# Scores paired by key halves of one sequence, the rows of odd heads by 64x64 quarters, one product with values moved a step forward

## The chip, the cores and the metric

One core of one Trainium2 chip. The metric is the time of one execution on the device in microseconds. Engine names are those of the profile: PE (TensorE matmuls, PEld its weight loads), DVE (VectorE), ACT (ScalarE), POOL (GpSimd), SP (SyncE, which issues DMAs here).

## The reference

Attention in which each score row keeps only the keys within `tau` of its maximum, then a mixture of experts in which each token goes to one expert. 8 batches, 8 heads, 576 positions, head size 64; 4608 tokens of width 512, 8 experts, hidden size 1024.

```python
scores = scale * np.matmul(q, k.transpose(0, 1, 3, 2))
scores = np.where(scores >= scores.max(-1, keepdims=True) - tau, scores, -1e9)
attn = softmax(scores)                       # over 576 keys
x = (attn @ v), heads side by side           # 4608 x 512
e_idx = argmax(x @ w_gate); gate_w = softmax(x @ w_gate)[e_idx]
out[token] = gate_w * sigmoid(x @ w_output_gate)[e_idx] * (relu(x @ w1[e_idx]) @ w2[e_idx])
```

## The kernel before

**Units and steps.** A unit `u` is one head of two sequences (`a` = 0, 1): 32 units. Two units, an even one and an odd one, make a group of nine steps (`STEPS`), 16 groups in all; step `t` of a group stands below as step 0 to 8. A step takes 128 queries of both sequences: steps 0 to 3 the four blocks of the even unit, steps 5 to 8 those of the odd unit, and step 4 the last 64 queries of both units and both sequences (`u is None` in the code).

**What a step does on each engine.** Step `g` issues, in an order that is written out in `Attention.run` and kept on PE, DVE, ACT and POOL:

- PE: the scores of step `g` into two PSUM tiles `ps[0]`, `ps[1]` (one for each sequence; a tile has two banks, and the two key halves `hf` of 288 keys lie in one bank each); in steps 0 and 4 the rows (`x_rows`: a finished head's output turned back to tokens, with the router's two products, 80 columns); in steps 1, 2, 3, 5, 6, 7, 8 a share of the product with values (`av_units`; ten products per head and half, shared out by the table `AV`); then the transposes of the probabilities of step `g - 2` (`remainder`, 2 products, and `blocks`, 16).
- DVE: two drains of the scores (L151, one for each sequence: scaled scores to SBUF, with the row extreme), then two masks of step `g - 1` (L178: threshold, product with the exponentials, row sums).
- ACT: two exponentials (L163), then the copies out of PSUM: the transposes of `remainder` (L229, L222) and of `blocks` (L254, in the step that transposes step 4's probabilities L248 and L250), the values' product (`X<-pa`, L273), in steps 0 and 4 the rows (L310, L312) between and after the exponentials.
- POOL: the threshold of the step (L156), sums, the rows' scaling (L322, L331), the router's scatters.

PSUM is full: `ps` has four banks and is used anew in every step, `pt` (the `blocks` transposes, L243) two banks and `pa` and `pr` one bank each, all in a single buffer. So PE's scores of a step wait for the drains of the step before, its `blocks` for ACT's copy of the last `blocks`, and a new product with values for ACT's copy of the last one.

**Operands.** fp32 products run as two passes. Queries and keys of a unit lie in one SBUF tile `qk`: sequence 0 on partitions 0 to 63, sequence 1 on partitions 64 to 127, so the two products that run side by side in the two row halves of the array are those of the two sequences, and both score tiles are finished at the end of the step's scores. `qk` has three buffers (`LB`), 608 KB each, loaded by one DMA on SP's queue, nine steps ahead.

**After the attention** the experts run on PE (lines from L968 on) with weights that SP's queue loads; eight of these loads are issued during the attention.

Of the kernel before, what the change touches and what calls it, by code (L numbers as in the profile page):

```python
# [8 lines left out]
F32 = mybir.dt.float32  # L9
# [12 lines left out]
class Attention:  # L22
    WU = 7
    SB = 4
    PB = 3
    LB = 3
    VB = 4
    STEPS = 9
    ENDS = 4
    WARM = {0: 4, 1: 2}  # L30
    AV = {1: (1, 0, 5), 2: (1, 5, 8), 3: (1, 8, 10), 5: (0, 0, 2), 6: (0, 2, 5), 7: (0, 5, 8), 8: (0, 8, 10)}
    PLACE = (2, 7)
    ROUTE = (2, 3, 6, 7, 8)

    def __init__(self, ctx, tc, ident, qkv, tau, wg, shape, router):
        self.tc, self.nc = tc, tc.nc
        nc = self.nc
        self.qkv = qkv
        self.B, self.H, self.S, self.D = shape
        self.NB = self.S // P  # L40
        self.M = self.NB * P
        self.R = self.S - self.M
        self.HS = self.S // 2
        self.KP = self.S + self.R
        self.QA = 2 * P
        self.NK = 2 * self.NB + 1
        self.nu = self.B // 2 * self.H
        self.router = router
        pool = lambda name, bufs, **kw: ctx.enter_context(tc.tile_pool(name=name, bufs=bufs, **kw))
        self.ld = pool("ald", self.LB)  # L50
        self.sp = pool("asp", 3)
        self.const = pool("aconst", 1)
        self.vld = pool("avld", self.VB)
        self.w2 = pool("aw2", 1)
        self.w3 = pool("aw3", 3)
        self.xp = pool("axp", 1)
        self.ps_s = pool("ps_s", 2, space=PSUM)
        self.ps_t = pool("ps_t", 1, space=PSUM)
        self.ps_a = pool("ps_a", 1, space=PSUM)
        self.ps_r = pool("ps_r", 1, space=PSUM)  # L60
        c = self.const
        self.ident = ident
        self.tau = c.tile([P, 1], F32, name="tau_sb")
        self.tau_in, self.wg_in = tau, wg
        warm = c.tile([P, 1], F32, name="warm")
        nc.vector.memset(warm, 0.0)
        nc.scalar.activation(warm, warm, AF.Exp)
        E2 = wg.shape[2]
        self.XW = self.D + E2
        self.wx = c.tile([P, self.H, self.XW], F32, name="wx")  # L70
        self.X = [c.tile([P, self.S + 64 * (1 - i)], F32, name=f"X{i}") for i in range(2)]
        self.half = [slice(0, 64), slice(64, P)]
        for pp in self.half:
            nc.gpsimd.tensor_copy(
                self.wx[pp, :, 0 : self.D], ident[pp, None, pp].broadcast_to([self.D, self.H, self.D])
            )
        nc.gpsimd.memset(self.X[0][0:64, self.S :], 0.0)
        self.loaded, self.sums, self.rinv, self.lt, self.sumup = {}, {}, {}, {}, None
        self.PTa, self.PTb, self.slot = {}, {}, 0

    def load_qk(self, u, first=False):
        nc, QW = self.nc, self.S
        x = self.ld.tile([P, QW + self.KP], F32, name="qk")
        src = self.qkv[u]
        if first:
            nc.sync.dma_start(x[:, QW:], src[:, QW : QW + self.KP])
            nc.sync.dma_start(x[:, 0:P], src[:, 0:P])
            nc.sync.dma_start(x[:, P:QW], src[:, P:QW])
        else:
            nc.sync.dma_start(x, src[:, 0 : QW + self.KP])  # L90
        self.loaded[u] = [x[:, 0:QW], x[:, QW:]]

    def load_v(self, u):
        v = self.vld.tile([P, self.NB * P + P], F32, name="vld")
        self.nc.sync.dma_start(v, self.qkv[u][:, self.S + self.KP :])
        self.loaded[u].append(v)

    def warm_up(self, n):
# [21 lines left out]
    def where(self, g):  # L120
# [2 lines left out]
            return s, None, self.NB  # L123
        return s, 2 * s + (i > self.ENDS), i - (self.ENDS + 1) * (i > self.ENDS)

    def scores(self, g, ps):
        nc, (s2, u, t) = self.nc, self.where(g)
        S, HS = self.S, self.HS
        c0 = 512 - HS
        for hf in range(2):  # L130
            cs = slice(c0 + hf * HS, c0 + hf * HS + HS)
            ks = lambda k0: slice(k0 + hf * HS, k0 + hf * HS + HS)
            if u is None:
                for i in range(2):
                    q, k = self.loaded[2 * s2 + i][0:2]
                    for a, pp in enumerate(self.half):
                        nc.tensor.matmul(
                            ps[i][self.half[a ^ i], cs], q[pp, self.M :], k[pp, ks(self.R * a)], start=True, stop=True
                        )
            else:  # L140
                q, k = self.loaded[u][0:2]
                for a, pp in enumerate(self.half):
                    nc.tensor.matmul(  # L143
                        ps[a][:, cs], q[pp, t * P : t * P + P], k[pp, ks(self.R * (1 - a))], start=True, stop=True
                    )
        mn = self.w3.tile([P, 2], F32, name="mn", bufs=4)
        ss = []
        SC = -(self.D ** -0.5)
# [106 lines left out]

    def av_units(self, u):
        nc = self.nc
        v = self.loaded[u][2]
        vm = v.rearrange("p (k a d) -> p k a d", a=2, d=64)
        X = self.X[u % 2]  # L260
        for half in range(2):
# [28 lines left out]
    def x_rows(self, u):  # L290
        X, pp, W, h = self.X[u % 2], self.half, self.XW, u % self.H
        ps = [pool.tile([P, 512], F32, name=name) for pool, name in ((self.ps_a, "pa"), (self.ps_r, "pr"))]
        mm = lambda out, c0, n, a: self.nc.tensor.matmul(
            out, X[pp[a], c0 : c0 + n], self.wx[pp[a], h], start=True, stop=True
        )
        last = slice(self.NB * W, self.NB * W + W)
        if u % 2:
            for a in range(2):
                mm(ps[0][pp[a], last], self.M, 64, a)
        for j in range(self.NB):  # L300
            for a in range(2):
                mm(ps[a][:, j * W : j * W + W], j * P, P, a)
        if u % 2 == 0:
            for a in range(2):
                mm(ps[a][:, last], self.M - 64 * a, P, a)
        return ps

    def x_copy(self, u, px, out, xl, a):
        nc, W = self.nc, self.XW
        nc.scalar.copy(xl[:, a::2], px[a][:, 0 : (5 - a) * W].rearrange("p (j w) -> p j w", w=W))  # L310
        if a and u % 2 == 0:
            nc.scalar.copy(xl[64:P, 8], px[1][64:P, 4 * W : 5 * W])  # L312
        if out:
            out(a)
# [32 lines left out]
    def run(self, hooks, begun):  # L347
# [4 lines left out]
        self.prep_first()  # L352
        for g in range(G + self.ENDS + 1):
            s, t = divmod(g, T)
            if t in (0, self.ENDS + 1) and s + 1 < ns:
                nxt = 2 * s + 2 + (t > 0)
                self.load_qk(nxt)
                self.load_v(nxt)
            g2 = g - 2
# [71 lines left out]
class Router:  # L431
# [71 lines left out]
    def init_units(self):  # L503
# [5 lines left out]
        for dst, group in parts:  # L509
            for r in range(0, dst.shape[0], P):  # L510
                ins = self.nc.sync.dma_start(dst[r : r + P, :], self.zrow)
                self.nodep(ins, group)
                self.init.append(ins)
                yield False

# [671 lines left out]
def lay_out(q, k, v, wg, wog):  # L1187
# [10 lines left out]
    vr = np.zeros((n, 2, r, 2, d), np.float32)  # L1198
    for a in range(2):
        vr[:, a, :, a] = vt[:, a, m:]  # L1200
    rows = lambda x: x.reshape(n, 2 * d, -1)
    qkv = np.concatenate(
        [rows(qt), rows(kt[..., m:]), rows(kt), vm, vr.reshape(n, 2 * r, 2 * d)], axis=2
    )
    e = wg.shape[1]
    w = np.zeros((2, d, h, 2, e), np.float32)
# [27 lines left out]
```

## Time and profile before

| | |
|---|---|
| median of 3 runs | 950.47 us (950.23 to 950.50) |
| profiled execution | 952.78 us, of which the span is 951.1 us |
| busy: PE, DVE, ACT, POOL | 98%, 71%, 64%, 33% of the span |
| granted clock of TensorE | 0.997 of full speed |
| attention | about the first 476 us |

The profiled execution is 2.3 us above the median of the runs; the span is that from its first to its last instruction. PE stands at 98%, but the ends of matmuls are modelled, so a busy PE also covers the time in which a product drains or the array changes its form. What the engines wait for is read from the waits and from the times at which instructions start.

### The profile page before, as it was taken

To read this page: it belongs to the slowest core of one execution; us is meant where nothing else is said; L and a number is where in the kernel's file an instruction comes from. 1 tells how busy PE (TensorE), PEld (TensorE's weight loads), DVE (VectorE), ACT (ScalarE), POOL (GpSimd) and SP (SyncE) were. 2 spreads that over 40 slices of the span, in tenths; PEclk is the share of its full clock that TensorE was granted. 3 is DMA by queue.
4 is the path that set the end of the run, shared out by engine and by line. 5 is a ranking of instruction groups with operands and counts; after the bars stand their busy time and mean duration, and the time that the engine had idled before them with its cause. 6 is when DMAs were issued, how large, how long until landed. Compare 5 with 4: busy or idle time off the path is not lost. (4 is left out here: it accounts for less than half of the span.)

```text
span 951.1 us, 21910 instructions
## 1 busy us (share of the span) xinstructions
PE 933.5 (98%) x8329; PEld 680.9 (72%) x8329; DVE 674.9 (71%) x1605; ACT 611.7 (64%) x1211; POOL 317.4 (33%) x568
## 2 busy tenths in 40 slices
PE   8999999999999999999999999999999999999996
PEld 4666666665666656666678887778878878878885
DVE  7899999999999999999965753435535535536621
ACT  6899898898988989889863332424424434436521
POOL 4344343456634576447626310202002002002001
PEclk9999999999999999999999999999999999999998
DMA  8972112123321233212247852526526426527301
GB/s 267 289 262 82 58 66 82 42 82 108 116 82 41 82 115 108 83 42 86 91 150 242 284 184 71 178 89 220 175 89 232 163 87 241 167 89 258 132 22 45
DMA packets 71402, 126.14 MB, mean 133 GB/s; under 512 B 8703, under 2 KB 35583, under 8 KB 71296
## 3 DMA queue, kind: packets, MB, share of 16 engines
q1 hardware_dynamic: 64656, 103.71, 34.3%
q0 software_dynamic: 6640, 21.02, 5.7%
q8 instruction: 66, 1.08, 0.5%
q14 instruction: 40, 0.33, 0.1%
HBM read 95.26 MB, written 30.22 MB: 132 GB/s over the span
## 5 line engine op out<-in xcount | busy, mean ns | idle before, releaser
L163 ACT ACTIVATE p<-s,mn 128x576 f32<-128x576 f32 x288 | 213.5, 782 | 45.3 <-DVE s L151 43.8
L178 DVE SCALAR_TENSOR_TENSOR p<-s,thr,p 128x576 f32<-128x576 f32 x288 | 231.2, 839 | 1.9 <-POOL thr L156 1.9
L151 DVE TENSOR_SCALAR_CACHE_REDUCE s<-ps 128x576 f32<-128x576 f32 x288 | 206.2, 753 | 33.2 <-PE ps L143 31.1
L1019 ACT ACTIVATE hh<-ph 128x512 fp32r<-128x512 f32 (+2 forms) x96 | 49.2, 512 | 205.1 <-PE ph L1016 199.8
L156 POOL TENSOR_SCALAR thr<-mn,tau_sb 128x2 f32<-128x2 f32 x144 | 97.5, 677 | 193.0 <-DVE s L151 190.0
L143 PE MATMUL ps<-qk 64*128 64x288 f32 x1024 | 155.9, 418 | 0.0
L1020 DVE SCALAR_TENSOR_TENSOR hl<-ph,hh 128x512 fp32r<-128x512 f32 (+2 forms) x96 | 55.5, 578 | 139.9 <-ACT hh L1019 136.5
L1014 PE MATMUL ph<-xh,w1h 128*128 128x512 f32 (+2 forms) x384 | 136.0, 354 | 0.0
L1016 PE MATMUL ph<-xh,w1l 128*128 128x512 f32 (+2 forms) x384 | 133.5, 348 | 0.2 <-issue 0.2
L1015 PE MATMUL ph<-xl,w1h 128*128 128x512 f32 (+2 forms) x384 | 133.4, 347 | 0.2 <-DVE xl L823 0.2
L1036 PE MATMUL py<-w2h,hh 128*128 128x512 f32 x304 | 120.3, 396 | 0.9 <-ACT hh L1019 0.9
L1038 PE MATMUL py<-w2h,hl 128*128 128x512 f32 x304 | 120.5, 396 | 0.6 <-DVE hl L1020 0.6
L811 POOL DMA_INDIRECT out_dram<-yo,kid x39 | 42.7, 1095 | 233.0 <-DVE yo L810 86.7
L1037 PE MATMUL py<-w2l,hh 128*128 128x512 f32 x304 | 120.0, 395 | 0.0
L269 PE MATMUL pa<-PTb,vld 128*64 128x320 f32 x640 | 101.3, 444 | 2.2 <-ACT X L273 1.5
L143 PEld LDWEIGHTS ps<-qk 64*128 64x128 f32 x1024 | 92.1, 188 | 14.5 <-DVE s L151 1.9
L243 PE MATMUL pt<-ident,p 64*128 64x64 f32 x2304 | 96.6, 223 | 3.5 <-ACT PTb L254 1.8
L243 PEld LDWEIGHTS pt<-ident,p 64*128 64x128 f32 x2304 | 83.5, 139 | 6.0 <-ACT PTb L254 4.9
L1014 PEld LDWEIGHTS ph<-xh,w1h 128*128 128x128 f32 x384 | 72.1, 188 | 11.9 <-issue 0.8
L823 DVE TENSOR_TENSOR w1l<-r,w1h 128x1024 fp32r<-128x1024 f32 x52 | 63.7, 1225 | 22.8 <-ACT w1h L820 21.9
L269 PE MATMUL pa<-PTa,vld 128*64 128x256 f32 x640 | 79.7, 387 | 0.0
L1015 PEld LDWEIGHTS ph<-xl,w1h 128*128 128x128 f32 x384 | 72.2, 188 | 10.1 <-DVE xl L823 0.6
(199 smaller groups left out, 1514.7 us busy)
## 6 DMA issues: line engine op xcount, KB each, us to landing
r<-in_moe_w_dram SPq DMA_DIRECT2D x104, 512.0 KB, 4.1
qk<-in_qkv_dram SPq DMA_DIRECT2D x31, 608.0 KB, 3.9
vld<-in_qkv_dram SPq DMA_DIRECT2D x32, 320.0 KB, 3.7
xs<-zrow SPq DMA_DIRECT2D x32, 257.0 KB, 8.2
xg<-xs SPq DMA_DIRECT2D x6, 1028.0 KB, 5.2
xg<-xs SPq DMA_DIRECT2D x4, 514.0 KB
xg<-xs SPq DMA_DIRECT2D x2, 771.0 KB
out_dram<-yo,kid POOLq DMA_INDIRECT x39
```

Of the source, the lines that this page charges most:

```text
L143: nc.tensor.matmul(ps[a][:, cs], q[pp, t * P : t * P + P], k[pp, ks(self.R * (1 - a))], start=True, stop=True)
L151: nc.vector.tensor_scalar(s, ps[a][:, c0 : c0 + S], SC, None, op0=ALU.mult, op1=ALU.min, accum_out=mn[:, a : a + 1])
L163: self.nc.scalar.activation(e, s, AF.Exp, bias=mn[:, a : a + 1], scale=-1.0)
L178: nc.vector.scalar_tensor_tensor(e, s, thr[:, a : a + 1], e, op0=ALU.is_le, op1=ALU.mult, accum_out=sums[a])
L243: nc.tensor.transpose(pt[:, o : o + 64], p[hs[h], k0 : k0 + P], id_[hs[h], hs[h]])
L269: nc.tensor.matmul(pa[self.half[a], 0:N], vm[:, kb, a], PT[:, 4 * a + kb if i else self.NK - 1], start=(i == 0), stop=(i == self.NB), skip ...
L1014: nc.tensor.matmul(ph, w1h[:, c, fs], self.xh[:, c, 0:N], start=(c == 0), stop=False)
L1015: nc.tensor.matmul(ph, w1h[:, c, fs], self.xl[:, c, 0:N], start=False, stop=False)
L1016: nc.tensor.matmul(ph, w1l[:, c, fs], self.xh[:, c, 0:N], start=False, stop=(c == 3))
L1036: nc.tensor.matmul(Y, hh[:, ts], wh, start=(f == 0), stop=False)
L1037: nc.tensor.matmul(Y, hh[:, ts], wl, start=False, stop=False)
L1038: nc.tensor.matmul(Y, hl[:, ts], wh, start=False, stop=(f == 7))
```

## The change

Six edits. (1) Each unit's queries are laid out twice, on both partition halves, and its keys by halves: key half 0 on partitions 0 to 63, key half 1 on 64 to 127. The two products that run side by side are now the two key halves of one sequence, and sequence 0's scores come before sequence 1's. (2) `qk` grows to 928 KB and has two buffers, and each unit is loaded five steps before its first use, not nine (`nxt`). The first unit is loaded in six pieces. (3) The rows of odd heads are made by products of 64 tokens, four quarters of the array side by side (20 products of 64x64 in place of 2 of 64x64 and 8 of 64x128), and their last 64 tokens of sequence 1 now need a copy of their own on ACT, as those of even heads do (L312). (4) `AV`: step 5 makes three of the ten steps of a head's first half and step 6 two; before it was two and three. (5) The zero rows that the router's buffer is filled with (`xs<-zrow`, 32 DMAs) each wait for a threshold on POOL, which spreads them over steps. (6) The layout of the input follows on the host.

```diff
-    LB = 3
+    LB = 2
-    AV = {1: (1, 0, 5), 2: (1, 5, 8), 3: (1, 8, 10), 5: (0, 0, 2), 6: (0, 2, 5), 7: (0, 5, 8), 8: (0, 8, 10)}
+    AV = {1: (1, 0, 5), 2: (1, 5, 8), 3: (1, 8, 10), 5: (0, 0, 3), 6: (0, 3, 5), 7: (0, 5, 8), 8: (0, 8, 10)}
...
+        b = [0, P, P + KH, S + KH, S + KH + P, self.QK - KH, self.QK]
+        for i in (1, 0, 5, 3, 2, 4) if first else ():
+            nc.sync.dma_start(x[:, b[i] : b[i + 1]], src[:, b[i] : b[i + 1]])
...
+    def operands(self, u, a, pp, q0, k0):
+        x, S, KH = self.loaded[u][0], self.S, self.KH
+        n = min(P, S - q0)
+        q0 += a * (S + KH) + (KH if q0 and not a else 0)
+        k0 += self.QK - KH if a else P
+        return x[pp, q0 : q0 + n], x[pp, k0 : k0 + self.HS]
...
-        for hf in range(2):
-            cs = slice(c0 + hf * HS, c0 + hf * HS + HS)
...
-                q, k = self.loaded[u][0:2]
-                for a, pp in enumerate(self.half):
-                    nc.tensor.matmul(
-                        ps[a][:, cs], q[pp, t * P : t * P + P], k[pp, ks(self.R * (1 - a))], start=True, stop=True
-                    )
+        for x in range(2):
+            for hf, pp in enumerate(self.half):
+                cs = slice(c0 + hf * HS, c0 + hf * HS + HS)
+                if u is None:
+                    for a in range(2):
+                        q, k = self.operands(2 * s2 + x, a, pp, self.M, self.R * a)
+                        nc.tensor.matmul(ps[x][self.half[a ^ x], cs], q, k, start=True, stop=True)
+                else:
+                    q, k = self.operands(u, x, pp, t * P, self.R * (1 - x))
+                    nc.tensor.matmul(ps[x][:, cs], q, k, start=True, stop=True)
...
+                if u % 2:
+                    for c in range(2):
+                        mm(ps[a][pp[c], cs], min(j * P + 64 * c, self.M), 64, a)
+                else:
+                    mm(ps[a][:, cs], j * P - 64 * (a and j == self.NB), P, a)
...
-        if a and u % 2 == 0:
+        if a:
             nc.scalar.copy(xl[64:P, 8], px[1][64:P, 4 * W : 5 * W])
...
-            if t in (0, self.ENDS + 1) and s + 1 < ns:
-                nxt = 2 * s + 2 + (t > 0)
+            nxt = 2 * s + 1 + (t > 0)
+            if t in (0, self.ENDS + 1) and 1 < nxt < nu:
...
                 self.nodep(ins, group)
+                self.behind(ins)
```

Three places in the order of instructions. On PE, steps 5 and 6 of a group before: the scores (L143), the share of the product with values (L269, counted in products of one sequence), the transposes (L208, L243).

```order
L143 MATMUL ps<-qk 128x288 x4
L269 MATMUL pa<-PTa,vld 64x256 x4
L208 MATMUL pr<-ident,p 128x64
L208 MATMUL pa<-ident,p 128x64
L243 MATMUL pt<-ident,p 128x64 x16
L143 MATMUL ps<-qk 128x288 x4
L269 MATMUL pa<-PTa,vld 64x256 x6
```

The same place now:

```order
L146 MATMUL ps<-qk 128x288 x4
L270 MATMUL pa<-PTa,vld 64x256 x6
L209 MATMUL pr<-ident,p 128x64
L209 MATMUL pa<-ident,p 128x64
L244 MATMUL pt<-ident,p 128x64 x16
L146 MATMUL ps<-qk 128x288 x4
L270 MATMUL pa<-PTa,vld 64x256 x4
```

Two products have gone from step 6 to step 5, ahead of step 5's transposes. On PE, the start of step 4 before (the scores, then the odd head's rows, of which the last two lines stand three times more):

```order
L243 MATMUL pt<-ident,p 128x64 x16
L137 MATMUL ps<-qk 64x288 x8
L293 MATMUL pa<-wx,X_215 64x80 x2
L293 MATMUL pa<-wx,X_215 128x80
L293 MATMUL pr<-wx,X_215 128x80
```

And now (the last two lines stand four times more):

```order
L244 MATMUL pt<-ident,p 128x64 x16
L143 MATMUL ps<-qk 64x288 x8
L294 MATMUL pa<-wx,X_215 64x80 x2
L294 MATMUL pr<-wx,X_215 64x80 x2
L294 MATMUL pa<-wx,X_215 64x80 x2
```

The rows' products all have the form of the scores ahead of them; the form changes after them, at the transposes. On SP's queue, the loads of the opening before, from the second unit's `qk` on (`vld` values, `xs<-zrow` zero rows, `sums<-swap` row sums moved between partitions):

```order
L90 DMA qk<-in_qkv_dram 128x1216
L95 DMA vld<-in_qkv_dram 128x640
L90 DMA qk<-in_qkv_dram 128x1216
L95 DMA vld<-in_qkv_dram 128x640 x2
L511 DMA xs<-zrow 128x514 x8
L90 DMA qk<-in_qkv_dram 128x1216
L511 DMA xs<-zrow 128x514 x6
L184 DMA sums<-swap 64x1 x2
```

And now (`r` are the first weights of the experts):

```order
L90 DMA qk<-in_qkv_dram 128x1856
L95 DMA vld<-in_qkv_dram 128x640 x3
L778 DMA r_7688<-in_moe_w_dram 128x4x256
L779 DMA r_7689<-in_moe_w_dram 128x2x512
L778 DMA r_7692<-in_moe_w_dram 128x4x256
L779 DMA r_7693<-in_moe_w_dram 128x2x512
L90 DMA qk<-in_qkv_dram 128x1856
L778 DMA r_7696<-in_moe_w_dram 128x4x256
```

The third unit's load no longer stands beside the second's; it now stands behind four loads of weights, and the zero rows come after it.

## Rows read from the trace of the kernel before

**Rows 1.** Stretch from group 2 to group 14: busy us (and instructions) of each engine.

```profile
59.70:443.60 383.90, 379.62 (x4768) 243.37 (x4766) 358.90 (x1030) 347.11 (x761) 194.52 (x317) 1.00 0.26 83
```

**Rows 2.** Waits: who for whom, us in total, times, longest.

```profile
DVE s L151 <- PE ps L143: 31.1, 50, 4.2
PEld pa L269 <- ACT X L273: 11.7, 24, 0.9
```

**Rows 3.** PE in time, steps 4 to 7 of group 3 (start, us).

```profile
102.30 1.20 PE L137 MATMUL ps<-qk 64*64 64x288 f32 x16
103.32 0.62 PE L293 MATMUL pa<-wx,X 64*64 64x80 f32 x5
103.62 0.33 PE L293 MATMUL pr<-wx,X 64*128 64x80 f32 x1
103.78 0.27 PE L293 MATMUL pa<-wx,X 64*128 64x80 f32 x1
...
104.56 0.22 PE L208 MATMUL pa<-ident,p 64*128 64x64 f32 x1
...
104.62 0.67 PE L243 MATMUL pt<-ident,p 64*128 64x64 f32 x16
105.12 1.19 PE L143 MATMUL ps<-qk 64*128 64x288 f32 x8
106.24 1.08 PE L269 MATMUL pa<-PTa,vld 128*64 128x256 f32 x8
107.26 0.27 PE L208 MATMUL pr<-ident,p 64*128 64x64 f32 x1
...
107.68 0.71 PE L243 MATMUL pt<-ident,p 64*128 64x64 f32 x16
108.23 1.19 PE L143 MATMUL ps<-qk 64*128 64x288 f32 x8
109.35 1.52 PE L269 MATMUL pa<-PTa,vld 128*64 128x256 f32 x12
...
111.47 1.19 PE L143 MATMUL ps<-qk 64*128 64x288 f32 x8
112.68 0.49 PE L269 MATMUL pa<-PTb,vld 128*64 128x320 f32 x2
```

**Rows 4.** DVE in time, the first drain of steps 3 and 4.

```profile
100.47 0.76 DVE L151 TENSOR_SCALAR_CACHE_REDUCE s<-ps 128x576 f32<-128x576 f32 x1 [0.45 <-PE ps L143]
...
103.54 0.76 DVE L151 TENSOR_SCALAR_CACHE_REDUCE s<-ps 128x576 f32<-128x576 f32 x1
```

**Rows 5.** ACT in time, steps 4 to 6 of group 3.

```profile
104.33 0.78 ACT L163 ACTIVATE p<-s,mn 128x576 f32<-128x576 f32 x1
...
106.17 0.42 ACT L310 COPY xl<-pr 128x320 f32<-128x320 f32 x1
...
106.58 1.04 ACT L254 COPY PTb<-pt 128x1024 f32<-128x1024 f32 x1
107.49 1.48 ACT L163 ACTIVATE p<-s,mn 128x576 f32<-128x576 f32 x2
...
109.03 1.07 ACT L254 COPY PTb<-pt 128x1024 f32<-128x1024 f32 x1
110.25 1.46 ACT L163 ACTIVATE p<-s,mn 128x576 f32<-128x576 f32 x2 [0.15 <-DVE s L151]
...
112.26 0.37 ACT L273 COPY X<-pa 128x256 f32<-128x256 f32 x1
```

**Rows 6.** ACT in time, an even head's rows (step 0 of group 4).

```profile
121.88 0.42 ACT L310 COPY xl<-pr 128x320 f32<-128x320 f32 x1
...
122.69 1.02 ACT L254 COPY PTb<-pt 128x1024 f32<-128x1024 f32 x1
```

**Rows 7.** PEld in time, a product with values behind scores, nothing late.

```profile
205.01 0.74 PEld L269 LDWEIGHTS pa<-PTb,vld 128*64 128x64 f32 x8 [0.39 <-issue]
```

**Rows 8.** DMA issues: KB each, median us to landing.

```profile
qk<-in_qkv_dram SPq DMA_DIRECT2D x31, 608.0 KB, 3.9
```

More of the change, by code (lines that the diff above doesn't have):

```diff
@@ L43, in __init__ @@
         self.HS = self.S // 2
-        self.KP = self.S + self.R
+        self.KH = self.HS + self.R
+        self.QK = 2 * self.S + 2 * self.KH
         self.QA = 2 * P
@@ L81, in load_qk @@
     def load_qk(self, u, first=False):
-        nc, QW = self.nc, self.S
-        x = self.ld.tile([P, QW + self.KP], F32, name="qk")
+        nc, S, KH = self.nc, self.S, self.KH
+        x = self.ld.tile([P, self.QK], F32, name="qk")
         src = self.qkv[u]
[L85 to L91, printed above, removed]
+        b = [0, P, P + KH, S + KH, S + KH + P, self.QK - KH, self.QK]
+        for i in (1, 0, 5, 3, 2, 4) if first else ():
+            nc.sync.dma_start(x[:, b[i] : b[i + 1]], src[:, b[i] : b[i + 1]])
+        if not first:
+            nc.sync.dma_start(x, src[:, 0 : self.QK])
+        self.loaded[u] = [x]
     def load_v(self, u):
         v = self.vld.tile([P, self.NB * P + P], F32, name="vld")
-        self.nc.sync.dma_start(v, self.qkv[u][:, self.S + self.KP :])
+        self.nc.sync.dma_start(v, self.qkv[u][:, self.QK :])
         self.loaded[u].append(v)
@@ L129, in scores @@
         c0 = 512 - HS
-        for hf in range(2):
-            cs = slice(c0 + hf * HS, c0 + hf * HS + HS)
[L132 to L135, printed above, removed]
-                    for a, pp in enumerate(self.half):
-                        nc.tensor.matmul(
-                            ps[i][self.half[a ^ i], cs], q[pp, self.M :], k[pp, ks(self.R * a)], start=True, stop=True
-                        )
-            else:
-                q, k = self.loaded[u][0:2]
-                for a, pp in enumerate(self.half):
-                    nc.tensor.matmul(
-                        ps[a][:, cs], q[pp, t * P : t * P + P], k[pp, ks(self.R * (1 - a))], start=True, stop=True
-                    )
+        for x in range(2):
[8 more added lines that the diff above has]
+                    nc.tensor.matmul(ps[x][:, cs], q, k, start=True, stop=True)
         mn = self.w3.tile([P, 2], F32, name="mn", bufs=4)
@@ L257, in av_units @@
         nc = self.nc
-        v = self.loaded[u][2]
+        v = self.loaded[u][1]
         vm = v.rearrange("p (k a d) -> p k a d", a=2, d=64)
@@ L295, in x_rows @@
         )
-        last = slice(self.NB * W, self.NB * W + W)
-        if u % 2:
+        for j in range(self.NB + 1):
+            cs = slice(j * W, j * W + W)
             for a in range(2):
[L299 to L305, printed above, removed]
+                if u % 2:
[3 more added lines that the diff above has]
+                    mm(ps[a][:, cs], j * P - 64 * (a and j == self.NB), P, a)
         return ps
@@ L1200, in lay_out @@
         vr[:, a, :, a] = vt[:, a, m:]
-    rows = lambda x: x.reshape(n, 2 * d, -1)
+    two = lambda x: np.concatenate([x, x], axis=1)
+    kh = lambda a: np.concatenate(
+        [kt[:, a, :, m:], kt[:, a, :, : s // 2], kt[:, a, :, s // 2 - r :]], axis=2
+    ).reshape(n, d, 2, -1).transpose(0, 2, 1, 3).reshape(n, 2 * d, -1)
     qkv = np.concatenate(
-        [rows(qt), rows(kt[..., m:]), rows(kt), vm, vr.reshape(n, 2 * r, 2 * d)], axis=2
+        [two(qt[:, 0, :, :P]), kh(0), two(qt[:, 0, :, P:]), two(qt[:, 1]), kh(1), vm, vr.reshape(n, 2 * r, 2 * d)],
+        axis=2,
     )
```

## The prediction

> **What bounds the kernel now.** I read the table of stretches first. From group 2 to group 14 PE is busy 379.6 of 383.9 us, DVE 358.9 and ACT 347.1 [rows 1]: PE sets the pace, but two engines follow at 93% and 90%, so what PE gives up they may take. Before a product with values the weight loads pause 0.39 us although nothing is late [rows 7]; it is the array changing its form, and counts as PE's own work. The list of waits then says who is late. DVE waits 31.1 us for scores; PE waits 24 times for the values' copy on ACT [rows 2], 11.7 us, of which 24 x 0.39 = 9.4 us would pass anyway. So 2.3 us of it are real.
>
> The steps have to be read one by one, since they differ. In group 3 I put down where PE's scores start: step 4 at 102.30, step 5 at 105.12, step 6 at 108.23, step 7 at 111.47 [rows 3]. Two places are not PE's own. In step 5 the `remainder` transposes start at 107.26 and `blocks` only at 107.68; in step 4 the second follows the first by 0.06 us (104.56, 104.62), after a change of form I take 0.05 more. ACT's copy of the last `blocks` ends at 106.58 + 1.04 = 107.62 [rows 5], and `blocks` starts 0.06 later: PE waits 0.3 us for ACT. In step 7 the product with values starts 1.21 us after the scores, in step 5 1.12 us after: it waits 0.09 us for the copy of X, which ends at 112.26 + 0.37 = 112.63 [rows 3, 5].
>
> Where does ACT lose that time? Step 4's exponentials start at 104.33, behind the drain that starts at 103.54 [rows 4, 5], and that one behind the scores of step 4, finished as a whole. The chain that ends last in steps 4 to 7 is: scores of step 4, drain, exponential, rows' copies, `blocks` copy, next exponentials, copy of X, product of step 7.
>
> **Scores by sequence.** Step 4's 16 products take 103.32 - 102.30 = 1.02 us, four rounds of 0.255. Before, both tiles were finished at the end; now `ps[0]` is finished after two rounds, 0.51 us sooner. The work on PE is the same: as many products, side by side in the same two row halves, and still in two banks. For DVE the drain of step 4 goes from 103.54 to 103.03 if DVE is free by then. It is: the drain of step 3 had waited 0.45 us for scores [rows 4], and moves by that too. So step 4's exponential goes from 104.33 to 103.82. From here on DVE runs about half a step's scores ahead of where it was.
>
> **The added copy on ACT.** For an even head the `blocks` copy starts 122.69 - 121.88 = 0.81 us after the second rows' copy [rows 6], for an odd head 106.58 - 106.17 = 0.41 [rows 5]. The copy that odd heads get costs 0.40 us, 15 times inside the attention, and it lies in the chain. So step 4's `blocks` copy moves by -0.51 + 0.40 = -0.11: it ends at 107.51.
>
> **Rows by quarters.** Before: 104.56 - 103.32 = 1.24 us [rows 3]. The 20 products are ten rounds of four, two passes each counted. Low bound: the scores' four quarters ran a round of 288 columns in 0.255; 80 columns make 0.071, ten rounds 0.71, and a change of form behind them for 0.16 (the first pair of the new form, 103.62 to 103.78; in the stream a pair takes (104.56 - 103.78) / 7 = 0.11): 0.87. High bound: a round takes as long as such a pair, and the sum is 1.26. I take the low one, since it comes from the same form. PE is up to 0.37 us ahead at the end of step 4.
>
> **The product moved.** 12 passes take 1.52 and 8 take 1.08 [rows 3]: 0.44 us goes from step 6 into step 5, where PE waits anyway. Step 5's `blocks` could start at 107.26 - 0.37 + 0.44 + 0.11 = 107.44; ACT lets it at 107.57. So step 6 begins 0.11 earlier (108.12), and step 7, with 0.44 less in step 6, at 111.47 - 0.11 - 0.44 = 110.92. PE would be ready for the product of step 7 at 110.92 + 1.12 = 112.04.
>
> ACT is not. It is busy without a break behind the `blocks` copy, so the next one goes from 109.03 to 108.92 and ends at 109.99. Exponentials start up to 0.13 before the listed end of the copy ahead (107.49 against 107.62); step 6's then start at 109.86 in place of 110.25. Their drain, 0.51 earlier, is no longer late. The copy of X ends 0.39 earlier at 112.24, and the product of step 7 starts at 112.29, not 112.68. That is **0.39 us a group**, of which ACT decides the size; PE has 0.25 to spare. In groups where DVE also does the router's work its drain decides, and the gain is up to 0.51. 15 groups x 0.4 = 6.0 us (5.9 to 7.7).
>
> **Steps 0 to 3.** PE's own work there is unchanged. What is left are the real waits, 2.3 us for X and a little for drains; with DVE and ACT half a scores' time ahead I take half of them as gone: 1.2 us (0 to 2.3).
>
> **The loads.** 928 KB in place of 608; by bytes 3.9 us to landing [rows 8] becomes 6.0. A load is issued when the scores of step 4 (or 8) are done and needed five steps later: in group 3 from 103.3 to beyond 111.47 + 2 x 2.8 = 117, 14 us. Hidden; without that cover each late load would cost its lateness, 30 times. In the opening the third unit's load stands behind four loads of weights; against that, the zero rows are now spread, which takes bytes away there. In the first scores half a tile is ready 0.51 sooner, against up to 2.1 us for the larger load; I take 0. The end of the attention (one more ACT copy, 0.37 less on PE) and the experts are left as they are.
>
> **Sum.** 6.0 + 1.2 = 7.2 us of the profiled span of 951.1 (943.9). The profiled execution is 952.78, 2.3 above the runs' median; taken off the median of 950.47 it makes **943.3 us**. Own range 940.5 (7.7 + 2.3) to 947.5 (half of the chain's gain, nothing else).
>
> **Rivals.** (a) The lead gets through whole. If ACT is faster behind the added copy than I let it be, PE's own work is the bound: per group 0.37 for the rows, 0.31 and 0.09 for the two waits, 15 x 0.77 = 11.6, with the 2.3 it is 936.6 us. For it: the ready times of ACT and PE lie 0.25 apart. Against: ACT is at 90% and every term of its chain is a measured row. 0.06.
>
> (b) The lead doesn't come, because DVE is held by something else at step 4, and the added copy remains. Step 4's `blocks` copy is 0.40 late, ends at 108.02; step 6 starts at 108.63, step 7 at 111.43; step 6's exponentials about 0.12 late, the product of step 7 at 112.80. 15 x 0.12 = 1.8: 952.3, with the rest of the kernel as it was; 950 to 952.3, no change. For it: DVE at 93%. Against: its two waits for scores just ahead. 0.14.
>
> (c) Slower: the quarters cost by the product and not by the round. Now 20 passes take 1.24 us, 0.062 each; 40 at that price are 2.48, with the change of form 2.64. `blocks` of step 5 then starts at 107.44 + 1.77 = 109.21, step 6 at 109.76, step 7 at 112.56, and the product of step 7 at 113.68, 1.0 us later than now: 15 us, 965.5. It turns the sign from 1.64 us for the rows on (0.04 a product). Against it: 16 `blocks` transposes fill 104.62 to 105.12, 0.031 each [rows 3]. 0.07. The Trainium skill, page "TensorE: Matmul & The Clock Gate", section "Wait — 56ns, not 53.3ns?", would speak for it: with hardware decode off, the sequencer spends about 62 ns on each matmul, and that bounds small ones. By that rule 40 products are 2.48 us and the sum is that of (c); the transposes at 0.031 don't agree with it, unless they stood in the queue already. (d) Loads late in the opening or in every unit: from 14 us to landing on; 0.03.
>
> **How the numbers follow.** Forecast 0.70, (a) 0.06, (b) 0.14, (c) and (d) 0.10. What a measurement here can tell from no change is about 0.2%, 1.9 us. The gains of the forecast and of (a) are all larger but for a few: faster 0.76, same 0.14, slower 0.10. The range of 8 in 10 runs from 938.0 (without most of (a)) to 950.0, into (b), and leaves out (c), (d) and half of (b).
>
> **What would show it.** Step 4's scores to its first drain about 0.75 us in place of 1.24; PE's rows of odd heads 0.85 to 0.95 us; three rows' copies on ACT in step 4; step 5's `blocks` no more than 0.2 behind its `remainder`; step 6 near 2.8 us; the product of step 7 0.2 to 0.4 us late behind ACT; a group near 29.0 us, which is 383.9 / 13 = 29.5 now [rows 1]. DVE's wait for scores falls from 31 us to under 15. Wrong would be: a drain of `ps[0]` that still starts at the end of the scores, rows over 1.64 us, or a scores' product that waits for a load.

## The result and the profile after

The changed kernel takes 940.37 us (median of 5 runs, 939.64 to 940.47) against 950.26 of the kernel before in the same comparison: ratio 0.9896, 95% interval 0.9885 to 0.9907, a gain of 9.9 us. Its profiled execution is 939.92 us, its span 938.2.

The table of stretches from group 2 to group 14, that of [rows 1]:

```profile
59.10:432.97 373.87, 370.30 (x5028) 239.69 (x5026) 357.69 (x1030) 351.24 (x775) 194.32 (x317) 1.00 0.38 122
```

A group takes 373.87 / 13 = 28.76 us, before 29.53. DVE does its work of before (1030 instructions) and ACT 14 copies more (775 instructions, before 761) in less time, so they now stand at 96% and 94%. The list of waits, beside [rows 2]:

```profile
DVE s L152 <- PE ps L146: 20.4, 37, 3.8
...
PEld pa L270 <- ACT X L274: 10.2, 16, 1.0
```

One row of the kernel before was not among those that the prediction used: the weight loads of the rows (L293), which also wait for the copy of X, 30 times:

```profile
PEld pa L293 <- ACT X L273: 10.6, 30, 0.4
```

By the trace 14 of the 30 stand in step 0, 0.38 us each, 15 in step 4, 0.33 us each, and one behind the last group. In the changed kernel the line is L294. The view of that line lists what it waited for:

```profile
its engine sat idle before it (us, times) until:
  ACT PTa L230: 0.6, 2
  ACT X L274: 0.3, 1
```

These three lie behind the last scores, from 461.9 us on. In the groups the wait has gone, and with it comes the part of the gain that was not forecast.

PE in time, steps 4 to 7 of group 3, the stretch of [rows 3]:

```profile
100.92 1.20 PE L143 MATMUL ps<-qk 64*64 64x288 f32 x16
101.94 0.23 PE L294 MATMUL pa<-wx,X 64*64 64x80 f32 x2
...
102.74 0.27 PE L209 MATMUL pa<-ident,p 64*128 64x64 f32 x1
...
103.35 1.19 PE L146 MATMUL ps<-qk 64*128 64x288 f32 x8
104.47 1.52 PE L270 MATMUL pa<-PTa,vld 128*64 128x256 f32 x12
105.92 0.27 PE L209 MATMUL pr<-ident,p 64*128 64x64 f32 x1
...
106.21 0.71 PE L244 MATMUL pt<-ident,p 64*128 64x64 f32 x16
106.76 1.19 PE L146 MATMUL ps<-qk 64*128 64x288 f32 x8
...
109.57 1.19 PE L146 MATMUL ps<-qk 64*128 64x288 f32 x8
110.91 0.49 PE L270 MATMUL pa<-PTb,vld 128*64 128x320 f32 x2 [0.15 <-ACT X L274]
```

Step 4 takes 2.43 us (before 2.82), step 6 2.81 (3.24); step 5 grows to 3.41 (3.11), since it has three products now. In step 5 `blocks` still starts 0.29 us behind `remainder`, where 0.11 would do, and in step 7 the product starts 1.34 us behind the scores, where 1.12 would do: PE still waits for ACT at both places. DVE's first drain of step 4, beside [rows 4], and ACT in the same step, beside [rows 5]:

```profile
101.70 0.76 DVE L152 TENSOR_SCALAR_CACHE_REDUCE s<-ps 128x576 f32<-128x576 f32 x1 [0.15 <-PE ps L143]
```

```profile
102.50 0.78 ACT L164 ACTIVATE p<-s,mn 128x576 f32<-128x576 f32 x1 [0.17 <-DVE s L152]
...
104.34 0.42 ACT L309 COPY xl<-pr 128x320 f32<-128x320 f32 x1
104.78 0.22 ACT L311 COPY xl<-pr 64x80 f32<-64x80 f32 x1
...
105.14 1.02 ACT L255 COPY PTb<-pt 128x1024 f32<-128x1024 f32 x1
...
110.49 0.36 ACT L274 COPY X<-pa 128x256 f32<-128x256 f32 x1
```

The drain starts 0.78 us behind the scores (1.24 before), and the `blocks` copy 0.80 us behind the rows' copy (0.41 before), with the added copy (L311) between them.

**Where the time went, step by step.** The next table is worked out from the traces. The length of a step is the time from its first scores product to that of the next step, and each number is a sum over groups 1 to 14, in us. The kernels below the second line are those of the experiments.

| kernel | step 0 | 1 to 3 | 4 | 5 | 6 | 7 | 8 | all |
|---|---|---|---|---|---|---|---|---|
| before | 39.9 | 149.9 | 39.5 | 44.6 | 45.3 | 52.5 | 41.5 | 413.1 |
| changed | 37.2 | 148.2 | 34.1 | 48.5 | 39.3 | 53.7 | 41.4 | 402.5 |
| b_xfirst | 39.8 | 149.2 | 39.4 | 44.1 | 45.3 | 52.4 | 41.5 | 411.6 |
| a_xfirst | 37.2 | 148.2 | 34.1 | 48.2 | 39.3 | 53.7 | 41.5 | 402.1 |
| a_nolead | 39.9 | 149.2 | 34.8 | 54.0 | 39.4 | 57.0 | 41.5 | 415.7 |
| a_nolead_xfirst | 39.9 | 149.2 | 34.8 | 54.1 | 39.4 | 57.1 | 41.5 | 416.0 |
| a_late8 | 46.2 | 148.3 | 34.1 | 48.2 | 39.3 | 53.7 | 41.5 | 411.3 |
| a_leadonly | 37.2 | 148.2 | 39.0 | 42.3 | 45.4 | 52.1 | 41.5 | 405.6 |
| a_rows128 | 37.2 | 148.2 | 39.0 | 44.5 | 39.4 | 55.6 | 41.5 | 405.3 |
| a_rows128_late | 37.2 | 148.2 | 39.0 | 44.5 | 39.4 | 52.8 | 41.5 | 402.5 |
| a_avold | 37.2 | 148.2 | 34.1 | 48.2 | 45.3 | 50.5 | 41.5 | 405.0 |
| a_poolmove | 37.7 | 148.2 | 35.9 | 46.1 | 41.5 | 67.0 | 43.9 | 420.3 |
| a_poolmove_late | 37.5 | 150.8 | 36.6 | 46.1 | 40.8 | 57.3 | 41.5 | 410.4 |
| a_best | 37.3 | 149.3 | 35.0 | 45.7 | 39.3 | 53.5 | 41.5 | 401.6 |

The profiled execution of before is 2.3 us above its median, so the b_xfirst row (949.52 us in its profile, and no different in time from before) is the better one to subtract from: steps 4 to 7 give 181.2 - 175.6 = 5.6 us, steps 1 to 3 1.0, step 0 2.6, together 9.2 in 14 groups, at that rate 9.9 in 15. Group 1 starts at 30.53 us, before at 30.50: the opening gave nothing. From the scores of the last step to the end of the span it is 479.6 us, in b_xfirst 479.0. The loads and the spread zero rows were not run apart; the sum leaves nothing over for them.

### The profile page after: what moved, and what is told of

Same layout as the page of the kernel before. It is cut to its first block, busy times and chain, and to the rows that moved or that the text cites. A ratio compares the mean times of both kernels' runs of the same rounds, so it can differ in the third digit from the quotient of the medians.

```text
span 938.2 us, 22582 instructions
## 1 busy us (share of the span) xinstructions
PE 919.6 (98%) x8649; PEld 674.9 (72%) x8649; DVE 674.0 (72%) x1605; ACT 616.6 (66%) x1227; POOL 318.4 (34%) x568
## 5 line engine op out<-in xcount | busy, mean ns | idle before, releaser
L179 DVE SCALAR_TENSOR_TENSOR p<-s,thr,p 128x576 f32<-128x576 f32 x288 | 231.4, 839 | 2.4 <-POOL thr L157 2.4
L152 DVE TENSOR_SCALAR_CACHE_REDUCE s<-ps 128x576 f32<-128x576 f32 x288 | 205.7, 750 | 22.5 <-PE ps L146 20.4
L146 PE MATMUL ps<-qk 64*128 64x288 f32 x1024 | 152.9, 417 | 0.3 <-DMA qk<-in_qkv_dram 0.3
L811 POOL DMA_INDIRECT out_dram<-yo,kid x39 | 44.1, 1130 | 231.8 <-DVE yo L810 85.1
L146 PEld LDWEIGHTS ps<-qk 64*128 64x128 f32 x1024 | 87.7, 189 | 16.2 <-DVE s L152 1.4
```

The lines of the kernel that those rows point to most:

```text
L146: nc.tensor.matmul(ps[x][:, cs], q, k, start=True, stop=True)
L152: nc.vector.tensor_scalar(s, ps[a][:, c0 : c0 + S], SC, None, op0=ALU.mult, op1=ALU.min, accum_out=mn[:, a : a + 1])
L179: nc.vector.scalar_tensor_tensor(e, s, thr[:, a : a + 1], e, op0=ALU.is_le, op1=ALU.mult, accum_out=sums[a])
```

## The experiments

### Why step 0 became shorter: a_late8, b_xfirst, a_xfirst

In step 0 the even head's rows follow the scores. Before, the weight load is held, here at the start of group 4, and the ACT row below it is the copy of X issued in step 8:

```profile
119.13 0.18 PEld L293 LDWEIGHTS pa<-wx,X 64*128 64x128 f32 x1 [0.38 <-ACT X L273]
```

```profile
118.64 0.44 ACT L273 COPY X<-pa 128x320 f32<-128x320 f32 x1
```

The copy ends at 119.08, the load starts 0.05 us later; so do all 30 loads of the list. In the changed kernel the same load is issued among the last scores, with ACT's copy over at 116.40 + 0.44 = 116.84:

```profile
117.03 0.19 PEld L294 LDWEIGHTS pa<-wx,X 64*128 64x128 f32 x1
```

```profile
116.40 0.44 ACT L274 COPY X<-pa 128x320 f32<-128x320 f32 x1
```

What the wait costs is seen in PE's own rows, the scores of step 0 and the first products of the rows into `pa`, before and now:

```profile
118.02 1.19 PE L143 MATMUL ps<-qk 64*128 64x288 f32 x8
119.13 0.33 PE L293 MATMUL pa<-wx,X 64*128 64x80 f32 x1
...
119.30 0.27 PE L293 MATMUL pa<-wx,X 64*128 64x80 f32 x1
```

```profile
116.24 1.19 PE L146 MATMUL ps<-qk 64*128 64x288 f32 x8
117.27 0.23 PE L294 MATMUL pa<-wx,X 64*128 64x80 f32 x1
...
117.34 0.27 PE L294 MATMUL pa<-wx,X 64*128 64x80 f32 x1
```

The first product starts 1.11 us behind the scores, now 1.03, and the second follows after 0.17 us, now 0.07. So of the 0.38 us that are listed, 0.18 are lost.

Was the pause PE's wait for ACT, or PE's own? **a_late8** makes the copy of X three times in step 8.

```diff
             elif done:
-                done()
+                for _ in range(3 if t == 8 else 1):
+                    done()
```

> The changed kernel with the copy of X made three times in step 8 (the same data, 2 x 0.32 us more on ACT there). Theory W (step 0's 0.18 us came from PE's wait, ahead of the even head's rows, for the last of ACT's copies out of the two tiles pa and pr): the rows of step 0 start 0.27 us later and their first pair loses 0.1, step 0 goes from 2.66 to 3.0 us, and the time to 940.4 + 15 x 0.37 = 946. Rival F (the pause ahead of the rows is PE's own): step 0 stays at 2.66 us; at most the later ACT shows elsewhere.

Measured: 949.19 us, ratio 0.9992 (0.9983 to 1.0001): nearly the whole gain is gone. Step 0 is 3.29 us, +0.63, and no other step moves. The three copies in its trace, and the load behind them (PE's row):

```profile
118.41 1.35 ACT L274 COPY X<-pa 128x320 f32<-128x320 f32 x3
```

```profile
119.81 0.33 PE L294 MATMUL pa<-wx,X 64*128 64x80 f32 x1 [0.37 <-ACT X L274]
```

They end at 119.76, and the rows start 0.05 us behind. Theory W stands; the size was off because two more copies of the same tile took 0.91 us, not 0.64.

**b_xfirst** and **a_xfirst** issue the copy of X ahead of the remainder copies, in the kernel before and in the changed one.

```diff
                 out = self.remainder(g2, pr[g2], (bank, self.pa), True, first)
-                if g == G - 1:
+                if done:
                     done()
+                    done = None
```

> The kernel before, with the copy of X on ACT issued ahead of the two remainder copies of its step (it starts some 0.2 us sooner; nothing else changes). Theory X (the 0.18 us that step 0 lost in the changed kernel were PE's wait for that copy, made in step 8): step 0 falls from 2.84 to about 2.66 us with the old scores order, step 7's 0.09 us wait goes too, and the time falls by 15 x (0.18 + 0.09) = 4 us, to 946. Rival F (the pause ahead of the rows is PE's own, the array changing its form or two score tiles finishing in one pair): step 0 stays at 2.84 us, only step 7 gains, 15 x 0.09 = 1.4 us, 949.

> The changed kernel with the copy of X issued ahead of the remainder copies. In step 7 the product with values waits 0.22 us for that copy, made in step 6. Theory A (ACT's place of the X copy is what still holds steps 4 to 7): the wait goes, step 7 is 3.5 us, 15 x 0.22 = 3.3 us, 937.1. Rival: the remainder copies, now some 0.35 us later, hold the next product with values or the drains, and nothing is gained: 940.4 or above.

Measured: b_xfirst 949.66 us, 0.9998 (0.9988 to 1.0007); a_xfirst 939.34, 0.9889 (0.9874 to 0.9904). Neither moved: step 0 stayed at 2.84 us, step 7 of a_xfirst at 3.71. That is what rival F said of step 0, but the trace of b_xfirst gives the reason. X is copied first now, and the load of the rows waits all the same, for another copy:

```profile
118.86 0.41 ACT L273 COPY X<-pa 128x320 f32<-128x320 f32 x1
...
119.26 0.22 ACT L229 COPY PTa<-pa 128x64 f32<-128x64 f32 x1
```

```profile
119.54 0.18 PEld L293 LDWEIGHTS pa<-wx,X 64*128 64x128 f32 x1 [0.37 <-ACT PTa L229]
```

The rows go into `pa` and `pr`, and those are free only when the remainder pieces have been copied out of them too (119.26 + 0.22 = 119.48). PE waits for the last of three copies, and their order doesn't change when the last one ends. The theory had named one copy too narrowly; what counts is when ACT is through with all three, and that the lead moves. Step 7 of a_xfirst is the same case, and came out as its rival said: the product starts at 110.70 us, 0.06 behind the last remainder copy (110.22 + 0.42).

### What the lead of the first score tile is worth: a_nolead, a_nolead_xfirst, a_leadonly

**a_nolead** keeps everything but pairs one product of each sequence again (key half 0 of one beside half 1 of the other), so that both tiles end together. **a_nolead_xfirst** adds the edit above.

```diff
-        for x in range(2):
-            for hf, pp in enumerate(self.half):
+        for r in range(2):
+            for x in range(2):
+                hf = x ^ r
+                pp = self.half[hf]
```

> The changed kernel with the same 288-column score products in another order: the pair that runs side by side is again one product of each sequence (key half 0 of one, half 1 of the other), so both score tiles are finished at the end. Layout, loads, rows and the table stay. Theory L (nearly the whole gain is the lead of the first tile): drains start 1.24 us after the scores in step 4, step 0 is back at 2.84 us, steps 4 to 7 at 12.8 to 12.9: 15 x (0.18 + 0.4 to 0.5) = 9 to 10 us, 949 to 951. Rival Q (quarters and the moved product make the gain of steps 4 to 7 without the lead): only step 0 goes back, 15 x 0.18 = 2.7 us, 943.

> As a_nolead, and the copy of X issued ahead of the remainder copies. Both score tiles finish in one pair, but X is ready sooner. Theory X: step 0 is 2.66 us although no tile finishes early, and steps 4 to 7 win up to 0.33 us from the earlier X in step 6: 15 x (0.18 + 0.33) = 7.6 us under a_nolead, about 943. Rival F: step 0 stays at 2.84 us, 5 us under a_nolead, about 946.

Measured: 957.17 us, ratio 1.0075 (1.0061 to 1.0089), and 955.53, 1.0058 (1.0044 to 1.0071): slower than before the change. Theory L falls short here: the lead carries more than the whole gain. In the table step 0 is back (39.9), step 5 is 54.0 and step 7 57.0. The waits:

```profile
DVE s L154 <- PE ps L148: 38.5, 58, 5.5
PEld pa L272 <- ACT X L276: 15.0, 22, 0.9
PEld pa L296 <- ACT X L276: 10.5, 30, 0.4
```

The last of them is the 10.6 us of the rows again. a_nolead_xfirst was expected at 943 and keeps a step 0 of 2.85 us, for the reason found in b_xfirst. In a quiet group steps 4 to 7 of a_nolead take 13.13 us, before 12.76. In step 5 of group 3 `remainder` starts at 110.42, and `blocks` 0.40 us behind it, held by ACT's copy:

```profile
109.74 1.02 ACT L257 COPY PTb<-pt 128x1024 f32<-128x1024 f32 x1
```

```profile
110.82 0.71 PE L246 MATMUL pt<-ident,p 64*128 64x64 f32 x16
```

So without the lead the added ACT copy passes through the chain; this is read from the rows, since no run takes the copy out of a_nolead. About 2 us more lie in the opening (group 1 starts at 32.50), which none of the runs explains.

**a_leadonly** is the other way round: the lead with its layout and loads, the rows and the table as before.

```diff
-    AV = {1: (1, 0, 5), 2: (1, 5, 8), 3: (1, 8, 10), 5: (0, 0, 3), 6: (0, 3, 5), 7: (0, 5, 8), 8: (0, 8, 10)}
+    AV = {1: (1, 0, 5), 2: (1, 5, 8), 3: (1, 8, 10), 5: (0, 0, 2), 6: (0, 2, 5), 7: (0, 5, 8), 8: (0, 8, 10)}
...
-                if u % 2:
-                    for c in range(2):
-                        mm(ps[a][pp[c], cs], min(j * P + 64 * c, self.M), 64, a)
...
+                mm(ps[0][pp[a], last], self.M, 64, a)
+        for j in range(self.NB):
+            for a in range(2):
+                mm(ps[a][:, j * W : j * W + W], j * P, P, a)
...
-        if a:
+        if a and u % 2 == 0:
             nc.scalar.copy(xl[64:P, 8], px[1][64:P, 4 * W : 5 * W])
```

> The changed kernel with the old rows of odd heads (no added ACT copy) and the old table: what is left is the scores order with its layout and loads. Theory L (the lead makes the gain): step 0 2.66, step 4 2.78, step 5 about 2.8 (two products, no wait), step 6 3.24, step 7 3.5 to 3.6: 12.3 to 12.5 us for steps 4 to 7 against 12.36, 940 to 942. Rival Q (quarters and table bring half of it): steps 4 to 7 stay at 12.76 as before the change, 946.4.

Measured: 942.73 us, 0.9925 (0.9912 to 0.9939). The lead, with its layout and its loads, gives 7.3 us. The quarters and the table add 2.4 on top of it (3.1 by the table of steps); without it, the kernel that has them is slower than before the change. The time is 0.7 us above the expected range: step 5 takes 3.02 us, not 2.8, since `blocks` still waits there for ACT, 0.33 us behind `remainder` (106.25):

```profile
105.49 1.04 ACT L255 COPY PTb<-pt 128x1024 f32<-128x1024 f32 x1
```

```profile
106.58 0.71 PE L244 MATMUL pt<-ident,p 64*128 64x64 f32 x16
```

### What sets steps 4 to 7 now: a_avold, a_rows128, a_rows128_late, a_poolmove, a_poolmove_late

**a_avold** is the changed kernel with the old table (the first lines of the diff above).

> The changed kernel with the old table (step 5 two products, step 6 three). Theory A: step 5's block transposes go on waiting for ACT, so step 5 stays at 3.41 us, step 6 is 0.44 longer (3.25), step 7 loses its 0.21 us wait, since ACT has the same time and PE comes later: 15 x (0.44 - 0.21) = 3.4 us, 943.8. Rival: only the sum of PE's work counts, no change, 940.4.

Measured: 941.93 us, 0.9919 (0.9905 to 0.9933). The steps of a quiet group came out as written (2.43, 3.41, 3.24, 3.50); in groups where the router works step 7 had waited longer and won more. The loss is 1.6 us between the medians and 2.5 in the table of steps, not 3.4; the interval overlaps that of the changed kernel, so the loss is shown by the traces alone.

**a_rows128** has the old rows (the second and third part of that diff), so PE has more to do and ACT less.

> The changed kernel with the rows of odd heads as before (8 products of 128 tokens and 2 of 64, no added ACT copy). PE has 0.37 us more in step 4, ACT 0.40 less. Theory A: step 4 is 2.80 us, step 5 loses its 0.18 us wait (3.23), step 6 is 2.81, step 7 loses its 0.21 (3.50): together 12.35 in place of 12.36, no change, 940 to 941: the quarters with their copy are worth nothing here. Rival Q (the quarters are what PE gains by): 15 x 0.37 = 5.6 us slower, 946.

Measured: 942.84 us, 0.9925 (0.9912 to 0.9939), between the two. Steps 4, 5 and 6 are 2.78, 3.18 and 2.81, nearly as written, but step 7 is 3.81 and not 3.50: with ACT 0.40 us ahead, something else is late. DVE in time, with the masks of step 4 (L179) and the first drain of step 6 (L152), and POOL's work on the rows, in group 3 of this kernel:

```profile
106.86 1.19 DVE L179 SCALAR_TENSOR_TENSOR p<-s,thr,p 128x576 f32<-128x576 f32 x1
107.97 0.98 DVE L179 SCALAR_TENSOR_TENSOR p<-s,thr,p 128x576 f32<-128x576 f32 x1
108.88 0.75 DVE L152 TENSOR_SCALAR_CACHE_REDUCE s<-ps 128x576 f32<-128x576 f32 x1
```

```profile
106.13 1.30 POOL L323 TENSOR_TENSOR rows<-xl,rinv 128x256 f32<-128x256 f32 x2 [1.14 <-ACT xl L311]
107.39 0.97 POOL L332 TENSOR_TENSOR ltx<-xl,rinv 128x144 f32<-128x144 f32 x1
```

A mask takes 0.81 us in steps 1 to 3 and 5 to 8 of this kernel. Beside POOL's products it takes 1.19 and 0.98, so the drains of step 6 start some 0.5 us late. **a_rows128_late** tries that: POOL does this work two steps later, in the 12 of 15 groups where the router can wait for it.

```diff
-                self.x_out(xu, xl)
+                later = xu % 2 and xu % self.H < self.H - 1
+                if later:
+                    self.held = xu, xl
+                else:
+                    self.x_out(xu, xl)
...
                 self.denominators(2 * s)
+                if self.held:
+                    self.x_out(*self.held)
+                    self.logits(*self.held)
+                    self.held = None
```

> a_rows128, with POOL's work on an odd head's rows two steps later in 12 of the 15 groups. Theory C: the first mask of step 4 falls from 1.19 to 0.81 us, the second from 0.97 to 0.81, step 6's drains start up to 0.5 us sooner, ACT's exponentials of step 6 up to 0.13 to 0.25 sooner (then ACT's own copy holds them), step 7 falls from 3.81 to about 3.6: 12 x 0.2 = 2.4 us, 940.4. Rival (ACT alone sets step 7): no change, 942.8.

Measured: 939.94 us, 0.9892 (0.9877 to 0.9907). The same three DVE rows:

```profile
106.64 0.81 DVE L179 SCALAR_TENSOR_TENSOR p<-s,thr,p 128x576 f32<-128x576 f32 x1
107.37 0.81 DVE L179 SCALAR_TENSOR_TENSOR p<-s,thr,p 128x576 f32<-128x576 f32 x1
108.36 0.76 DVE L152 TENSOR_SCALAR_CACHE_REDUCE s<-ps 128x576 f32<-128x576 f32 x1 [0.17 <-PE ps L146]
```

Both masks are short, the drain waits for scores, and step 7 is 3.54 us. Theory C stands. POOL's work now lies beside a mask of step 6, which takes 0.97 us by it, but step 8 stays as long as it was (41.5 in the table). This kernel, without the quarters and without their ACT copy, is as fast as the changed one (402.5 us in both rows of the table): what the quarters save on PE can be had by moving POOL's work.

**a_poolmove** leaves the quarters and takes the added copy off ACT: ACT copies five columns at once into a tenth column, and POOL moves half of it on. (The tile of the opening's idle products is halved and read twice, to make room.)

```diff
-        nc.scalar.copy(xl[:, a::2], px[a][:, 0 : (5 - a) * W].rearrange("p (j w) -> p j w", w=W))
+        nc.scalar.copy(xl[:, a::2], px[a][:, 0 : 5 * W].rearrange("p (j w) -> p j w", w=W))
         if a:
-            nc.scalar.copy(xl[64:P, 8], px[1][64:P, 4 * W : 5 * W])
+            nc.gpsimd.tensor_copy(xl[64:P, 8], xl[64:P, 9])
```

> The changed kernel without the added ACT copy: ACT copies all five columns of sequence 1's rows into a tenth column (some 0.07 us more), and POOL moves the half column on from there, for even heads too. ACT gets some 0.33 us back in step 4 (and in step 0). Theory A (ACT's chain still sets steps 4 to 7): the 0.18 us wait of step 5's block transposes and the 0.21 us of step 7's product shrink, 0.33 to 0.39 us a group, 15 x 0.35 = 5 us, 935. Rival P (PE's own work or DVE's drains are the bound now): nothing, 940.4.

Measured: 960.62 us, 1.0116 (1.0100 to 1.0131), far from both. Step 5 lost its wait (3.18), but step 7 went to 4.28: the first mask of step 4 takes 1.30 us in group 3, and the next threshold stands behind more work on POOL. **a_poolmove_late** adds the edit of a_rows128_late.

> a_poolmove, with POOL's work on an odd head's rows (the half column, the two products of the rows, the logits' product) issued two steps later, behind the threshold and the denominators of step 6, in 12 of the 15 groups. There it should lie beside DVE's drains of step 7. Theory C (a_poolmove lost because POOL's work and DVE's masks of step 4 lay side by side: the first mask took 1.30 us in place of 0.81 and the threshold of step 5 stood behind it): the masks of step 4 are 0.81 to 0.85 again, step 5 stays at 3.18, step 7 falls from 4.28 to about 3.6: 12 x 0.65 = 8 us under a_poolmove, 953, and 12 x 0.3 under the changed kernel but for what the other three groups and step 0 lose. Rival (the masks are slow for another reason, or POOL's five-column work hits the next masks as hard): step 7 stays above 4.1, 958 to 961.

Measured: 949.75 us, 0.9992 (0.9983 to 1.0001). In the quiet groups it came out as written: the masks are 0.81, step 5 3.18, step 7 3.64, the group 28.26 us against 28.57 in the changed kernel. On ACT the `blocks` copy of step 4 starts 0.48 us behind the rows' copy, 0.80 in the changed kernel:

```profile
103.86 0.49 ACT L309 COPY xl<-pr 128x400 f32<-128x400 f32 x1
...
104.34 1.04 ACT L255 COPY PTb<-pt 128x1024 f32<-128x1024 f32 x1
```

So 0.32 us less on ACT and POOL's work out of the way of DVE are together worth 0.31 a group. Of this 0.23 lie in step 5, which was 3.18 us in a_poolmove too and so comes from ACT; the 0.08 in step 7 may come from either. The loss is in groups 8 and 12, which take 35 and 34 us; there, as in a_poolmove, even heads and the last head of a pair of sequences have POOL's copy ahead of a threshold.

### A version from these: a_best

a_best gives the copy to POOL in the 12 groups alone, late; the other places stay as in the changed kernel.

> The changed kernel with ACT's added half-column copy given to POOL in the 12 groups alone in which POOL's work on the odd head's rows can stand behind step 6's threshold; even heads and the last head of a pair of sequences keep the ACT copy and their place. Theory (a_poolmove_late lost its gain in the groups where POOL's copy stood ahead of a threshold beside the router's scatters, not in the others): the quiet groups take 28.26 us as there, against 28.57 in the changed kernel, the others are as in the changed kernel, and the time is 940.4 - 12 x 0.31 = 936.7. Rival (the late POOL work itself costs those groups): 945 or above.

Measured: 941.21 us against 952.90 of before on that chip: 0.9874 (0.9858 to 0.9891). On the 950.26 us of the first comparison that is 938.3, where 936.7 was expected. The quiet groups are 28.26 us as written, but groups 7, 8, 11 and 12, where the router works on a finished pair of sequences, take 0.2 to 0.8 us more than in the changed kernel (step 4 of group 7 takes 2.91, step 2 of group 8 3.98). The interval overlaps that of the changed kernel (0.9885 to 0.9907), so that it is faster is not shown. Why those groups lose stays open.

## Why the prediction came out as it did

The direction, the mechanism and the size of its main term held. The time lies 2.9 us under the likeliest value, for one step, and 0.1 under the forecast's own range. That it lies in the range of 8 in 10 (938.0 to 950.0) is in part luck: the lower end was set for rival (a), which did not come, and not for what did.

**Scores by sequence.** The first drain of step 4 was to start about 0.75 us behind the scores: 0.78. Step 4's `blocks` copy was to move by -0.11: measured from the scores of step 4 it ended at 5.32 [rows 3, 5] and ends at 106.16 - 100.92 = 5.24, so -0.08. a_nolead shows that this is the step on which all else rests.

**Steps 4 to 7, 15 x 0.4 = 6.0 us.** A quiet group went from 12.76 to 12.37; by the table it is 5.6 us in 14 groups, 0.40 each. That ACT decides the size is borne out for step 5 by a_poolmove and a_poolmove_late (0.32 off ACT, 0.23 gained there), with a limit that the prediction had not seen: DVE stands close behind, and POOL's work slows it (a_rows128).

**The added copy, the quarters, the moved product.** 0.40 was 0.39 (0.80 - 0.41). The rows take 0.80 us, not 0.87, from 101.94 to 102.74: a round of four passes comes every 0.069 us. Rival (c) is out: 40 passes at 0.062 would have been 2.48. The rule of the Trainium skill that stood beside it (page "TensorE: Matmul & The Clock Gate", section "Wait — 56ns, not 53.3ns?": some 62 ns a matmul with hardware decode off) is not what bounds this trace, where a pass of the rows costs 0.020 us; whether that was off, no run here shows. The moved product was worth 1.6 to 2.5 us (a_avold), within what its 0.44 a group can give.

**The step that failed: the real waits of steps 0 to 3.** The prediction put them at "2.3 us for X and a little for drains" and took half, 1.2 us; they gave 2.6 + 1.0 in 14 groups, 3.9 at that rate in 15. Steps 1 to 3 fit the 1.2. Step 0 was put at nothing, and it gave 0.18 us in every group, 2.8 in 15. PE's own work there was unchanged, as written, but the 2.3 us count the wait for X ahead of the products with values alone [rows 2]. The rows' loads wait for the same copy in the same list, and the prediction names no reason for leaving them out. It had read one pause of the loads, ahead of a product with values, as "the array changing its form" [rows 7]. Ahead of such a product that fits the changed kernel too, where the loads still pause with nothing late, 0.39 us each:

```profile
PEld pa L270 <- issue: 18.5, 48, 0.4
```

In steps 3 and 8, where nothing is late, the first such product starts 1.12 us behind the scores; the rows, in the same form as the scores, start 1.03 behind them. Ahead of the rows the pause was a wait for ACT, as the 0.05 us behind each copy's end and a_late8 show. With step 0's 2.8 us the sum would have been 7.2 + 2.8 = 10.0. The row of the list alone would not have given that number: of the 0.38 us listed in step 0, 0.18 came back, and of the 0.33 in step 4 only 0.04 (2.82 us before, 2.78 in a_leadonly, which has the old rows).

**Signs that missed.** DVE's wait for scores fell to 20.4 us, not under 15: the first drains of steps 3 and 8 of group 3 still wait 0.45 and 0.57 us for scores, before 0.45 and 0.54; DVE starts sooner there, and is through sooner. Step 5's `blocks` starts 0.29 behind `remainder`, not 0.2, and the rows take 0.80 us, not 0.85 to 0.95.

**Rivals.** (a) is not what happened: its 0.77 a group for steps 4 to 7 was 0.40, and both waits for ACT are still there, though the time lies at the edge of the forecast's own range (940.5). (b), no lead, was put at 952.3, +0.12 a group; a_nolead gives +0.37 in steps 4 to 7 and 957.17 in all. There the late `blocks` copy passes on to the scores of step 6, their drain and the exponentials behind it, where (b) let ACT catch up. (d): PE waited 0.3 us for queries and keys in all, its weight loads 0.8; the loads are hidden.

## What to carry to other kernels

When two tiles are finished together and drained one after the other, look first whether one of them can be finished early: here that cost PE nothing (step 4's scores take 1.02 us before and after) and moved the engines behind it. Before a pause is called the array's own, compare it with each line of the list of waits that names the same engine: a pause of 0.39 us with nothing late stood before one kind of product, and one of 0.38, a wait for ACT, before another. And what one engine is spared can be lost at the next one behind it: in a_rows128 part of what ACT's 0.40 us gave in step 5 was lost in step 7, until POOL's work was moved out of DVE's way.

## What the runs showed of the hardware

DVE's masks, which read two operands from SBUF, take 0.81 us alone and, where they lie beside POOL's products of the rows, up to 1.23 before the change, 1.19 in a_rows128 and 1.50 in a_best; the drains, which read PSUM, never took more than 0.76 us. Beside the masks of step 4 POOL's two products took 1.30 us in a_rows128, as they do two steps later in a_rows128_late, so there it is DVE that gives way; in some groups of a_poolmove POOL's second product takes 1.24 to 1.34 us in place of 0.73, so it can be either. Moving POOL's work by two steps brought the masks of step 4 back to 0.81 in the groups concerned (a_rows128_late, a_poolmove_late). The Trainium skill has this, page "SBUF — State Buffer", section "Who interferes with whom": a DVE instruction with two SBUF inputs contends with a GpSimd instruction that reads SBUF. The traces agree.

Copies by ACT of the same data into the same tile, one right behind the other, start 0.46 us apart (a_late8: 1.35 us for three), while a copy into another tile starts 0.32 us after the last of them.

What PE does behind an ACT copy that it waited for starts 0.05 to 0.06 us after the copy's listed end, in each of the cases above.
